# Retention and mixture of depths: the first batch's choice of rows ahead of other loads, its MLP from step 7 in place of step 10

## The chip, the cores and the metric

One core of a Trainium2 chip. The time is the device time of one execution in microseconds; several runs are taken and their median is given. The core's engines work side by side: TensorE (PE, its weight loads are PEld), VectorE (DVE), ScalarE (ACT), GpSimd (POOL) and SyncE (SP), which issues the direct DMA transfers. Each engine takes its instructions in the order in which they are written, and semaphores order them against each other.

## What is computed

Eight batches of 576 rows. The first part is retention: attention without softmax, in which a score is scaled by a power of a factor of its head. The second chooses 128 rows of each batch by a gate score and adds an MLP's result to them.

```python
# retention, B=8 H=8 S=576 D=64
scores = (1/sqrt(D)) * q @ k.T
gamma  = 1 - 2**(-5 - arange(H))
ret    = scores * where(i >= j, gamma**(i - j), 0)
x      = (ret @ v) as (B, S, 512)
# mixture of depths, capacity 128
score  = x @ w_gate
top    = the 128 rows of each batch with the largest score
ye     = relu(x[top] @ w1) @ w2          # 512 -> 1024 -> 512
out    = x;  out[top] += sigmoid(score[top]) * ye
```

## The kernel before

**Steps.** A batch is 9 chunks of 64 rows. A step takes two chunks, so the whole is 36 steps (`NS`) of two chunks in the order of the batches; step 4 (`(NC - 1) // 2`) holds the last chunk of batch 0 and the first of batch 1. A step loads one tile `raw` of 1 MB (q, k, v and natural k for both chunks), tile 0 in two halves. POOL scales v to `vs` (`scaled`). The matmuls of a step are two streams woven together by `matmuls(s)`, two of each in turn: `diagonal(s)` makes the scores `sc_ps` and adds to the running state `u_ps` (copied to `st` by ACT), and `crosswise(s - 1)` makes `y_ps` of the step before, from the masked scores `am` (DVE, `masked`) and the state. One round of four is called an iteration; a full step has 16.

**After the matmuls of a step** come `values(s - 1)` (scale `y_ps` to `xs`, in eight small ACT instructions for the steps in `BUSY`, otherwise in one DVE instruction; then two dot products with the gate's weights on DVE) and `stored(s - 2)`, the stores of `xs` to the output.

**The choice of rows.** When a batch's scores are there, `flatten` (DVE) and `spread` (a matmul with ones and a copy by ACT) lay them out as one `row` on all partitions. `compare` (DVE) counts for each row how many are ahead of it, `one_hot` (DVE) turns the ranks into a selection `hot`, `fetch` turns it into row numbers `idx` by five small matmuls and gathers these rows of the output as `xr` with an indirect DMA on POOL. For batch 0 (and the last two) the first six chunks are laid out and compared ahead of the last three. `gates` makes the sigmoid factor.

**The MLP.** `mlp(b)` transposes `xr` (`turn`, four transposes, then a copy) and puts eight parts on a list: four `up` (16 pairs of matmul passes each) and four `down`. `some(n)` issues n parts at the end of a step; n is chosen so that the list is empty when the next batch is `ready`. The last part scatters the result by an indirect DMA.

**The order around the change** is written by hand. Dictionaries hold what to do in a step: `inner[(s, i)]` before iteration i of the step's matmuls, `first` after them, `soon` and `mid` after `values`, `late` and `then` after the parts of the MLP. TensorE, DVE, ACT and SP follow the order of the program text; POOL's order is left to the scheduler. For batch 0 before:

```python
plan(inner, (s + 1, 12), spread, b, last)          # s = 5
for j in js:
    plan(first, s + 1 + int(j > 2), compare, b, j, last)
plan(first, s + 2, one_hot, b)
plan(inner, (s + 3, 4), fetch, b)
plan(inner, (s + 5, 4), mlp, b)
plan(inner, (s + 5, 13), some, 1)
ready.append(s + 5)
```

**When loads go out.** `pe` counts TensorE's instructions. Each time the count passes the edge of a block of 256 (by `SURE`, 8, more), at most one due piece of the weights (512 KB) and one `raw` tile go out, and only behind the matmul at that place (`behind`); a tile only while fewer than four are loaded ahead of the step (`lead`). With 64 matmuls of four instructions to a step, an edge falls once in about each step. Five tiles are loaded before the first step. The eight pieces of w1 and w2 are due from step 5 to step 12.

Of the kernel before, what the change touches and what calls it, by code (L numbers as in the profile page):

```python
# [21 lines left out]
BEFORE = 65  # L22
SURE = 8
ET = mybir.EngineType
ENGINES = {ET.PE, ET.DVE, ET.Activation, ET.SP}


def layout(NC, HG, cap):
# [11 lines left out]
def kernel(  # L40
# [23 lines left out]
    nc = tc.nc  # L64
    NS = qkvk.shape[0]
    DM = w1.shape[0]
# [4 lines left out]
    NC = 2 * NS // B  # L71
# [3 lines left out]
    W = HG * D  # L75
# [5 lines left out]
    loads = ctx.enter_context(tc.tile_pool(name="loads", bufs=8))  # L81
    work = ctx.enter_context(tc.tile_pool(name="work", bufs=3))
# [8 lines left out]
    chunk = lambda s, a: divmod(2 * s + a, NC)  # L91
    four = lambda ap: ap.rearrange("p (a h d) -> p a h d", a=2, h=HG)

    raw, weights = {}, deque()
    now = {"at": BEFORE, "edge": BLOCK, "load": 0, "step": 0, "quiet": 0}

    def load(behind=None):
        s, now["load"] = now["load"], now["load"] + 1  # L100
        raw[s] = x = loads.tile([P, 4, DM], F32, name="raw")
        n = 4 if s else 2
        for a in range(0, 4, n):
            start(x[:, a : a + n, :],
                  qkvk[s, :, DM * a : DM * (a + n)].rearrange("p (a e) -> p a e", a=n), behind)

    def start(out, in_, behind):
        ins = nc.sync.dma_start(out=out, in_=in_)  # L108
        if behind is not None:
            tc.add_manual_dep(ins.ins, behind.ins.name, mybir.DependencyInfo(  # L110
                mybir.DependencyClass.Sync, mybir.DependencyReason.DATA), reason="behind a fetch")

    def pe(ins, n=4):

        now["at"] += n
        if now["at"] >= now["edge"] + SURE:
            now["edge"] += BLOCK
            lead = now["load"] - now["step"]
            if now["quiet"] and lead > 2:
                now["quiet"] -= 1  # L120
                return ins
            due = weights and weights[0][0] <= now["step"]
            if due:
                start(*weights.popleft()[1:], ins)
            if now["load"] < NS and lead < 4:
                load(ins)
        return ins
# [7 lines left out]

    ctx.enter_context(tc.manual_schedule(engines=ENGINES))
    table = const.tile([P, col["end"]], F32, name="table")
# [16 lines left out]
    for f in range(0, FB, 2):  # L154
        e = slice(P * f, P * f + 2 * P)
# [5 lines left out]
    dec = table[:, : 2 * (NC + 1) * HG].rearrange("p (s c h) -> p s c h", s=2, c=NC + 1)  # L161
# [9 lines left out]
    for _ in range(3):  # L171
# [7 lines left out]

    BUSY = [s for s in range(1, (NC - 1) // 2 + 3) if s != (NC - 1) // 2]
    vs, am, sc_ps, y_ps, u_ps, st, xs, sc = {}, {}, {}, {}, {}, {}, {}, {}
    factor = lambda s, i: dec[:, i, chunk(s, 0)[1] : chunk(s, 0)[1] + 2, :].unsqueeze(3).to_broadcast(
        [P, 2, HG, D])
# [62 lines left out]
    def matmuls(s):  # L248
        a = diagonal(s) if s < NS else iter(())
        b = crosswise(s - 1) if s else iter(())  # L250
        for i in count():
            for f, more in inner.get((s, i), []):
                f(*more)
            some = [f for f in (next(a, None), next(a, None), next(b, None), next(b, None)) if f]
            if not some:
                return
            for f in some:
                f()
# [7 lines left out]
    def values(s):  # L266
        xs[s] = work.tile([P, DM], F32, name="xs", bufs=5)
        if s in BUSY:
            c = chunk(s, 0)[1]
            for a in range(2):  # L270
                for h in range(HG):
                    nc.scalar.activation(out=xs[s][:, hd[a][h]], in_=y_ps[s][:, hd[a][h]],  # L272
                                         func=AF.Copy, scale=dec[:, 1, c + a, h : h + 1])
        else:
            nc.vector.tensor_tensor(out=four(xs[s]), in0=four(y_ps[s]), in1=factor(s, 1),  # L275
                                    op=OP.mult)
        for a in range(2):
# [8 lines left out]
    def stored(s):  # L286
        (b, c), (b1, _) = chunk(s, 0), chunk(s, 1)
        for i, half in enumerate(halves):
            e = slice(W * i, W * i + W)
            if b == b1:  # L290
                nc.sync.dma_start(
                    out=outs[b][C * c : C * c + P, e].rearrange("(a t) e -> t a e", a=2),
                    in_=xs[s][half, :].rearrange("p (a e) -> p a e", a=2))
                continue
            nc.sync.dma_start(out=outs[b][C * c :, e], in_=xs[s][half, :W])
            nc.sync.dma_start(out=outs[b1][:C, e], in_=xs[s][half, W:])

# [123 lines left out]

    inner, first, soon, mid, late, then, ready, parts = {}, {}, {}, {}, {}, {}, [], deque()

    def mlp(b):
        turn(b)
        parts.extend((up, (b, f, 2)) for f in range(0, FB, 2))
        parts.extend((down, (b, part)) for part in range(4))
# [6 lines left out]
    def plan(when, s, f, *a):  # L436
        when.setdefault(s, []).append((f, a))

    for b in range(B):
        end = cuts(b)  # L440

        there = [(NC * b + c - 1) // 2 + 1 for c in end[1:]]
        last = len(there) - 1
        for part, s in enumerate(there):
            plan(soon, s, flatten, b, part)
        for part, s in enumerate(there[:-1]):
            plan(mid, s + 1, spread, b, part)
            for j in own(b, part):
                plan(then if b < B - 1 else mid, s + 1 + int(b == 0 and j > 1), compare, b, j, part)
        if b == B - 1:  # L450
            break
        s = there[-1]
        js = [*range(own(b, last).start), *own(b, last)]
        if b == 0:


            plan(inner, (s + 1, 12), spread, b, last)
            for j in js:
                plan(first, s + 1 + int(j > 2), compare, b, j, last)
            plan(first, s + 2, one_hot, b)  # L460
            plan(inner, (s + 3, 4), fetch, b)
            plan(inner, (s + 5, 4), mlp, b)
            plan(inner, (s + 5, 13), some, 1)
            ready.append(s + 5)
            plan(then, s + 5, gates, b)
            continue


        if last:
            when = 1, (1, 1, 1, 1, 2), 2, 3, 4  # L470
        elif b == 1:
# [15 lines left out]
    for s in range(NS + 1):  # L487
        now["step"] = s
        now["at"] += 1.5
        if s == 1:  # L490
            nc.sync.dma_start(out=wg, in_=spread_out(0, DM, P))
        while now["load"] < min(NS, s + 2):
            load()
        if s + 1 < NS:
            scaled(s + 1)
        matmuls(s)
        if s > 1:
            stored(s - 2)
        for f, a in first.get(s, []):
            f(*a)  # L500
        if s:
            values(s - 1)
        if s == 1:
            nc.vector.tensor_copy(out=place, in_=table[:, col["place"] : col["end"]])
        for f, a in soon.get(s, []) + mid.get(s, []):
            f(*a)

        n = -(-len(parts) // max(1, min([r for r in ready if r > s], default=s + 1) - s))
        some(n if s < NS else len(parts) - 1)
        for f, a in late.get(s, []) + then.get(s, []):  # L510
            f(*a)
    stored(NS - 1)

    b, part = B - 1, len(cuts(B - 1)) - 2
    spread(b, part)
# [72 lines left out]
```

## Time and profile before

| what | value |
|---|---|
| median of 3 runs | 265.66 us (261.38 to 268.25) |
| profiled run, span | 258.1 us |
| PE busy | 225.4 us, 87% of the span |
| DVE busy | 151.2 us, 59% |
| POOL / ACT busy | 59.6 / 59.3 us, 23% each |
| mean granted clock of TensorE | 0.965 |
| moved by DMA | 56.95 MB, mean 221 GB/s |
| gather of batch 0: issue, use by the transposes | 45.41 us, 53.41 us |

In the profile a slice's digit is the busy share in tenths. A gap in front of a group of instructions is given in brackets with what released it; "issue" means that the engine waited for nothing that the profile shows. The shares of busy time are means over stages with different limits: here an early stage with many loads, a long middle in which MLP parts fill the steps, and a tail with the last batch's choice and MLP.

### The profile page before, as it was taken

Reading aid. Unit: us, or ns where it says so; the run is one execution under the profiler, and the core shown is the slowest. Engines: PE = TensorE matmul, PEld = TensorE weight load, DVE = VectorE, ACT = ScalarE, POOL = GpSimd, SP = SyncE. Lnnn points to the kernel's source line nnn. Section 1 sums busy time; section 2 is a strip of 40 time slices with the busy share of each in tenths; the row PEclk is TensorE's granted clock in tenths of the full one; section 3 lists DMA queues with packets and bytes.
Section 4 is the critical chain, followed back from the end, with each engine's and each line's share of the span. In section 5 each row is a group of like instructions: output and inputs, shape, how many; then the busy total and the mean of one; then the engine's idle time right before and its main releaser. Section 6 shows DMA issues by size and latency. Waiting matters only on the chain.

```text
span 258.1 us, 11373 instructions
## 1 busy us (share of the span) xinstructions
PE 225.4 (87%) x5102; PEld 174.8 (68%) x5102; DVE 151.2 (59%) x436; ACT 59.3 (23%) x178; POOL 59.6 (23%) x59
## 2 busy tenths in 40 slices
PE   8565785689889989896999999999999999999991
PEld 3564574579755887555985799568966895784940
DVE  0156788542885536973983699579944861950201
ACT  1125443112510223112221321122211220211200
POOL 3333113312141112133131150413312210101101
PEclk9889979759999999999999999999999999999999
DMA  6999899998666776881778985888876303111101
GB/s 210 403 324 341 260 339 372 379 390 273 212 226 226 234 266 229 289 283 64 235 241 288 301 288 169 263 259 296 285 251 227 99 17 80 44 41 41 43 0 41
DMA packets 20945, 56.95 MB, mean 221 GB/s; under 512 B 2336, under 2 KB 13984, under 8 KB 16416
## 3 DMA queue, kind: packets, MB, share of 16 engines
q1 hardware_dynamic: 19616, 52.02, 59.9%
q0 software_dynamic: 1280, 4.20, 4.6%
q8 instruction: 40, 0.66, 1.0%
q14 instruction: 9, 0.07, 0.1%
HBM read 44.67 MB, written 11.53 MB: 218 GB/s over the span
## 4 chain that ended last, share of the span: by engine, by line
PE 51%; issue 24%; DMA 20%; POOL 2%; POOLq 1%; SPq 0%; DVE 0%
PE h_ps L134 14%; DMA raw<-in_qkvk 10%; PE ye_ps L134 9%; PE u_ps L134 8%; DMA xr<-out,idx 8%; PE sc_ps L134 8%; PE y_ps L134 7%; PE row_ps L134 3%; DMA w_sb<-in_w 2%; PE xg_ps L394 1%; POOL out L419 1%; POOL xr L375 1%; POOL vs L189 1%; POOLq L584 0%; SPq L108 0%
## 5 line engine op out<-in xcount | busy, mean ns | idle before, releaser
L189 POOL TENSOR_TENSOR vs<-raw,table 128x512 f32<-128x512 f32 x36 | 40.1, 1113 | 140.2 <-DMA raw<-in_qkvk 105.1
L134 PE MATMUL h_ps<-xg,w_sb 128*128 128x128 f32 x512 | 61.9, 280 | 0.1
L134 PEld LDWEIGHTS h_ps<-xg,w_sb 128*128 128x128 f32 x512 | 59.6, 195 | 2.2 <-issue 1.2
L134 PE MATMUL ye_ps<-w_sb,hT 128*128 128x512 f32 x128 | 60.1, 605 | 0.0
L134 PE MATMUL u_ps<-vs,raw 64*64 64x64 f32 x1024 | 45.9, 229 | 7.3 <-POOL vs L189 3.1
L262 DVE TENSOR_TENSOR am<-sc_ps,table 128x512 f32<-128x512 f32 x36 | 24.8, 688 | 45.5 <-PE sc_ps L134 26.5
L134 PE MATMUL y_ps<-vs,am 64*64 64x64 f32 x1152 | 46.1, 229 | 5.3 <-issue 4.8
L134 PEld LDWEIGHTS u_ps<-vs,raw 64*64 64x64 f32 x1024 | 37.8, 140 | 18.6 <-issue 12.8
L134 PE MATMUL sc_ps<-raw 64*64 64x64 f32 x1152 | 45.3, 228 | 4.4 <-issue 4.1
L134 PEld LDWEIGHTS sc_ps<-raw 64*64 64x64 f32 x1152 | 40.4, 143 | 9.2 <-issue 7.9
L209 ACT COPY st<-u_ps 128x256 f32<-128x256 f32 x64 | 24.0, 375 | 90.0 <-PE u_ps L134 59.9
L134 PEld LDWEIGHTS y_ps<-vs,am 64*64 64x64 f32 x1152 | 39.5, 141 | 5.4 <-issue 4.8
L134 PE MATMUL y_ps<-st,raw 64*64 64x64 f32 x1024 | 39.9, 226 | 0.9 <-issue 0.8
L283 DVE SCALAR_TENSOR_TENSOR scr<-xs,wg_half 128x256 f32<-128x256 f32 x72 | 34.8, 483 | 6.6 <-ACT xs L272 4.1
L350 DVE SCALAR_TENSOR_TENSOR scr<-row,tok,ahead 128x576 f32<-128x576 f32 (+2 forms) x49 | 36.2, 739 | 2.8 <-ACT row L326 0.8
L134 PEld LDWEIGHTS ye_ps<-w_sb,hT 128*128 128x128 f32 x128 | 22.7, 190 | 21.1 <-issue 20.1
L134 PEld LDWEIGHTS y_ps<-st,raw 64*64 64x64 f32 x1024 | 35.8, 141 | 1.3 <-issue 1.2
L275 DVE TENSOR_TENSOR xs<-y_ps,table 128x512 f32<-128x512 f32 x31 | 21.1, 682 | 7.4 <-PE y_ps L134 7.4
L406 ACT ACTIVATE hT<-h_ps 128x256 f32<-128x256 f32 x32 | 12.3, 384 | 49.1 <-PE h_ps L134 49.1
L343 DVE SCALAR_TENSOR_TENSOR scr<-row,table 128x128 f32<-128x128 f32 (+1 forms) x40 | 12.7, 317 | 14.9 <-ACT row L326 14.2
L418 DVE SCALAR_TENSOR_TENSOR o<-ye_ps,gate,xr 128x512 f32<-128x512 f32 x8 | 6.0, 750 | 24.4 <-issue 12.7
L419 POOL DMA_INDIRECT out<-o,idx x8 | 9.0, 1130 | 35.2 <-DVE o L418 32.5
(32 smaller groups left out, 106.2 us busy)
## 6 DMA issues: line engine op xcount, KB each, us to landing
raw<-in_qkvk SPq DMA_DIRECT2D x35, 1024.0 KB, 5.4
out<-xs SPq DMA_DIRECT2D x64, 128.0 KB, 5.5
w_sb<-in_w SPq DMA_DIRECT2D x8, 512.0 KB, 6.5
raw<-in_qkvk SPq DMA_DIRECT2D x2, 512.0 KB
out<-xs SPq DMA_DIRECT2D x16, 64.0 KB, 6.3
wg<-in_w_gate SPq DMA_DIRECT2D x1, 256.0 KB
table<-in_consts SPq DMA_DIRECT2D x1, 130.5 KB
wg_half<-in_w_gate SPq DMA_DIRECT2D x2, 64.0 KB, 7.3
```

What stands on the lines that cost most here:

```text
L134: return pe(nc.tensor.matmul(out, lhsT, rhs, **more), 4 if lhsT.dtype == F32 else 2)
L189: nc.gpsimd.tensor_tensor(out=four(vs[s]), in0=four(raw[s][:, 2, :]), in1=factor(s, 0), op=OP.mult)
L209: nc.scalar.copy(out=st[b, c], in_=u_ps[b][:, :W])
L262: nc.vector.tensor_tensor(out=am[s], in0=sc_ps[s].rearrange("p (h d) -> p h d", h=H), in1=causal.unsqueeze(1).to_broadcast([P, H, C]), op= ...
L275: nc.vector.tensor_tensor(out=four(xs[s]), in0=four(y_ps[s]), in1=factor(s, 1), op=OP.mult)
L283: nc.vector.scalar_tensor_tensor(scr[:, :W], part, 1.0, wg_half, op0=OP.mult, op1=OP.mult, accum_out=sc[b][:, c : c + 1])
L343: nc.vector.scalar_tensor_tensor(scr[:, :n], row[b][:, P * j : P * j + n], 1.0, eye[:, :n], op0=OP.mult, op1=OP.mult, accum_out=tok[b][:, ...
L350: nc.vector.scalar_tensor_tensor(scr[:, : i1 - i0], row[b][:, i0:i1], tok[b][:, j : j + 1], ahead[:, at + i0 : at + i1], op0=OP.subtract, ...
L375: nc.gpsimd.indirect_dma_start(out=xr[b], out_offset=None, in_=outs[b], in_offset=bass.IndirectOffsetOnAxis(ap=idx[b][:, :1], axis=0))
L406: nc.scalar.activation(out=hT[b][:, f : f + n, :], in_=t[:, :n, :], func=AF.Relu)
L418: nc.vector.scalar_tensor_tensor(o, ye[b], gate[b], xr[b], op0=OP.mult, op1=OP.add)
L419: nc.gpsimd.indirect_dma_start(out=outs[b], out_offset=bass.IndirectOffsetOnAxis(ap=idx[b][:, :1], axis=0), in_=o, in_offset=None)
```

## The change

It puts the choice of batch 0 first. In steps 2 to 5 only half a tile goes out at each block edge, in place of a whole tile (and weights from step 5). The choice is made in steps 4 to 6: the row of the first part in the middle of step 4, the last chunk's values and stores as soon as they are there, the rest of the row and all comparisons within step 6. Two tiles and two weight pieces are sent together at the start of step 6, while DVE compares. The rows are fetched in step 7, and the MLP of batch 0 starts at the end of step 7 in place of step 10, with its eight parts spread over steps 7 to 14. For the later batches the fetch moves behind the step's MLP parts, and the MLPs of batches 1 and 2 come a step later. POOL's order is now written out too, `scaled` stands after the matmuls of a step, and `BUSY` reaches to step 12.

```diff
-ENGINES = {ET.PE, ET.DVE, ET.Activation, ET.SP}
+ENGINES = {ET.PE, ET.DVE, ET.Activation, ET.SP, ET.Pool}
...
+    DONE = (NC - 1) // 2
+    edges = deque([[], [(DONE + 1, 0)], [(DONE + 1, 1)], [(DONE + 2, 0)], [(DONE + 2, 1)],
+                   [], []])
...
+    def half_load(s, i, behind=None):
+
+        if s not in raw:
+            raw[s] = loads.tile([P, 4, DM], F32, name="raw")
+        start(raw[s][:, 2 * i : 2 * i + 2, :],
+              qkvk[s, :, 2 * DM * i : 2 * DM * (i + 1)].rearrange("p (a e) -> p a e", a=2), behind)
+        now["load"] = s + i
...
             now["edge"] += BLOCK
+            now["last"] = ins
+            if edges:
+                for s, i in edges.popleft():
+                    half_load(s, i, ins)
+                return ins
...
-    BUSY = [s for s in range(1, (NC - 1) // 2 + 3) if s != (NC - 1) // 2]
+    BUSY = [s for s in range(1, DONE + 9) if s != DONE]
...
+    def ahead_of(n):
+
+        for _ in range(n):
+            load(now["last"])
+            start(*weights.popleft()[1:], now["last"])
...
-            plan(mid, s + 1, spread, b, part)
+            if b:
+                plan(mid, s + 1, spread, b, part)
+            else:
+                plan(inner, (s + 1, 8), spread, b, part)
...
-            plan(inner, (s + 1, 12), spread, b, last)
+            plan(inner, (s + 1, 4), spread, b, last)
             for j in js:
-                plan(first, s + 1 + int(j > 2), compare, b, j, last)
-            plan(first, s + 2, one_hot, b)
-            plan(inner, (s + 3, 4), fetch, b)
-            plan(inner, (s + 5, 4), mlp, b)
-            plan(inner, (s + 5, 13), some, 1)
-            ready.append(s + 5)
-            plan(then, s + 5, gates, b)
+                plan(inner, (s + 1, 10), compare, b, j, last)
+            plan(inner, (s + 1, 10), one_hot, b)
+            plan(inner, (s + 1, 0), ahead_of, 2)
+            plan(inner, (s + 2, 4), fetch, b)
+            plan(mid, s + 2, mlp, b)
+            plan(mid, s + 2, ahead_of, 1)
+            ready.append(s + 2)
+            plan(then, s + 3, gates, b)
             continue
...
         elif b == 1:
-            when = 1, (1, 1, 1, 2, 2), 2, 3, 4
+            when = 1, (1, 1, 1, 2, 2), 2, 3, 5
         else:
-            when = 1, (1, 1, 2, 2, 3), 3, 4, 5 + int(b > 2)
+            when = 1, (1, 1, 2, 2, 3), 3, 4, 6
...
-        plan(mid, s + when[3], fetch, b)
+        plan(mid if last else late, s + when[3], fetch, b)
...
+        matmuls(s)
         while now["load"] < min(NS, s + 2):
             load()
         if s + 1 < NS:
             scaled(s + 1)
-        matmuls(s)
         if s > 1:
-            stored(s - 2)
+            for span in spans(s - 2)[int(s - 2 == DONE) :]:
+                stored(s - 2, span)
         for f, a in first.get(s, []):
             f(*a)
+        span, *more = spans(s - 1)
         if s:
-            values(s - 1)
+            values(s - 1, span)
+        if s - 1 == DONE:
+            stored(s - 1, span)
...
-        for f, a in soon.get(s, []) + mid.get(s, []):
+        for f, a in soon.get(s, []):
+            f(*a)
+        if s and more:
+            values(s - 1, *more)
+        for f, a in mid.get(s, []):
             f(*a)
```

More of the change, by code (lines that the diff above doesn't have):

```diff
@@ L96 @@
     raw, weights = {}, deque()
+    DONE = (NC - 1) // 2
+    edges = deque([[], [(DONE + 1, 0)], [(DONE + 1, 1)], [(DONE + 2, 0)], [(DONE + 2, 1)],
+                   [], []])
     now = {"at": BEFORE, "edge": BLOCK, "load": 0, "step": 0, "quiet": 0}
-    def load(behind=None):
-        s, now["load"] = now["load"], now["load"] + 1
+    def half_load(s, i, behind=None):
[4 more added lines that the diff above has]
+        now["load"] = s + i
+    def load(behind=None):
+        s = now["load"]
+        if s == 0 or s in raw:
+            for i in range(int(s in raw), 2):
+                half_load(s, i, behind)
+            return
         raw[s] = x = loads.tile([P, 4, DM], F32, name="raw")
[L102 to L105, printed above, removed]
+        start(x, qkvk[s].rearrange("p (a e) -> p a e", a=4), behind)
+        now["load"] = s + 1
     def start(out, in_, behind):
@@ L264, in masked, with spans, values @@
             in1=causal.unsqueeze(1).to_broadcast([P, H, C]), op=OP.mult)
-    def values(s):
-        xs[s] = work.tile([P, DM], F32, name="xs", bufs=5)
+    def spans(s):
+        return [range(2)] if chunk(s, 0)[0] == chunk(s, 1)[0] else [range(1), range(1, 2)]
+    def values(s, span):
+        if s not in xs:
+            xs[s] = work.tile([P, DM], F32, name="xs", bufs=5)
+        b, c = chunk(s, span.start)
         if s in BUSY:
-            c = chunk(s, 0)[1]
-            for a in range(2):
+            for a in span:
                 for h in range(HG):
                     nc.scalar.activation(out=xs[s][:, hd[a][h]], in_=y_ps[s][:, hd[a][h]],
-                                         func=AF.Copy, scale=dec[:, 1, c + a, h : h + 1])
+                                         func=AF.Copy, scale=dec[:, 1, c + a - span.start, h : h + 1])
         else:
-            nc.vector.tensor_tensor(out=four(xs[s]), in0=four(y_ps[s]), in1=factor(s, 1),
-                                    op=OP.mult)
-        for a in range(2):
+            part = slice(span.start, span.stop)
+            nc.vector.tensor_tensor(out=four(xs[s])[:, part], in0=four(y_ps[s])[:, part],
+                                    in1=factor(s, 1)[:, part], op=OP.mult)
+        for a in span:
             b, c = chunk(s, a)
@@ L284, in values, with stored @@
                                            op1=OP.mult, accum_out=sc[b][:, c : c + 1])
-    def stored(s):
-        (b, c), (b1, _) = chunk(s, 0), chunk(s, 1)
+    def stored(s, span):
+        (b, c), n = chunk(s, span.start), len(span)
         for i, half in enumerate(halves):
             e = slice(W * i, W * i + W)
[L290 to L296, printed above, removed]
+            nc.sync.dma_start(
+                out=outs[b][C * c : C * (c + n), e].rearrange("(a t) e -> t a e", a=n),
+                in_=xs[s][half, W * span.start : W * span.stop].rearrange("p (a e) -> p a e", a=n))
     flat, row, tok, rank, hot = {}, {}, {}, {}, {}
@@ L511 @@
             f(*a)
-    stored(NS - 1)
+    for span in spans(NS - 1):
+        stored(NS - 1, span)
     b, part = B - 1, len(cuts(B - 1)) - 2
```

## The prediction, with its working

> **What bounds the kernel now.** I read the slices of the page first, then windows over the early part, then the waits of the matmul engine, then its single gaps in the timeline, and last the engines that release those gaps.
>
> ```profile
> PE   8565785689889989896999999999999999999991
> PEclk9889979759999999999999999999999999999999
> DMA  6999899998666776881778985888876303111101
> GB/s 210 403 324 341 260 339 372 379 390 273 212 226 226 234 266 229 289 283 64 235 241 288 301 288 169 263 259 296 285 251 227 99 17 80 44 41 41 43 0 41
> ```
>
> One slice is 258.1 / 40 = 6.45 us. From about 122 us TensorE is 90% busy or more: what is left there is work. What can be won lies before. Up to 60 us TensorE is 50 to 80% busy while DMA moves 260 to 400 GB/s, and there is a hole in slice 18 (116 to 122 us).
>
> ```profile
> 15.00:18.90 3.90, 2.32 (x128) 2.07 (x129) 2.47 (x6) 0.84 (x3) 1.04 (x1) 1.00 0.86 295
> 49.00:59.40 10.40, 8.88 (x171) 8.01 (x171) 5.64 (x14) 1.23 (x3) 1.74 (x3) 0.51 1.01 374
> ```
>
> The columns are the stretch, its length, busy time of PE, PEld, DVE, ACT, POOL, granted clock, DMA share, GB/s. The first row is step 2: 2.32 us of matmuls in 3.9 us. The second shows that the clock is at half from 49 to 59.4 us, over the very start of the first MLP.
>
> ```profile
> PE y_ps L134 <- issue: 4.4, 4, 1.8
> PE sc_ps L134 <- issue: 3.7, 3, 1.6
> PE idx_ps L134 <- DVE hot L360: 3.0, 2, 1.9
> PE u_ps L134 <- issue: 2.6, 5, 0.6
> ```
>
> These are the waits of the first 75 us. "Issue" is 10.7 us in 12 gaps. Gaps over 0.15 us between 12 and 60 us add up to 14.5 us; three of them and a later one, by the timeline:
>
> ```profile
> 25.25 0.27 PE L134 MATMUL y_ps<-vs,am 64*64 64x64 f32 x1 [1.84 <-issue]
> 43.66 0.36 PE L134 MATMUL idx_ps<-place,hot 128*128 128x1 f16 x5 [1.89 <-DVE hot L360]
> 53.41 1.12 PE L394 MATMUL xg_ps<-table,xr 128*128 128x128 f32 x4 [0.84 <-DMA xr<-out,idx]
> 118.62 0.66 PE L394 MATMUL xg_ps<-table,xr 128*128 128x128 f32 x4 [2.87 <-DMA xr<-out,idx]
> ```
>
> The long issue gaps (1.08, 1.07, 1.84, 1.26, 1.07, 1.57 us) stand about 256 instructions apart; those of 0.5 us stand at the start of a step and end when `am` of the step before is ready. So a step is 2.1 us of matmuls + 0.5 us for `am` + about 1.2 us for instructions, 3.7 to 3.9 us.
>
> [...] The page agrees on the blocks (10,204 TensorE instructions, 40 packets and 0.66 MB on the instruction queue)[...]. [...] The gather agrees: 3.3 us at best, 8.0 us at 45 us, with all of DMA in use. [...] The trace agrees: half clock at about 11 to 14.6, 32 to 35.4 and 49 to 59.4 us, one, one and three windows.
>
> **The change, part by part.**
>
> *Fewer loads in steps 2 to 5.* Half a tile (512 KB) at each of four block edges in place of 1 MB, then at steps 5 and 6 1 MB and 0.5 MB of weights. With 0.25 MB of stores a step then moves 0.75 MB, some 2 us of DMA at 390 GB/s, in place of 3.2 us or more, so a fetch finds free engines. I take the fetch gaps of steps 3 to 5 as gone (1.07, 1.84, 1.26 us). Step 2 keeps its gap, since the first five loads run until 17 us. So step 3 begins at 18.9 us as before, step 4 at 21.0 instead of 22.1.
>
> *The row of the first six chunks moves into step 4 (iteration 8).* Its input is late:
>
> ```profile
> 25.00 0.56 DVE L311 TENSOR_TENSOR flat<-sc,table 128x384 f32<-128x384 f32 x1
> 36.15 0.41 DVE L350 SCALAR_TENSOR_TENSOR scr<-row,tok,ahead 128x192 f32<-128x192 f32 x1
> 40.38 0.28 DVE L343 SCALAR_TENSOR_TENSOR scr<-row,table 128x128 f32<-128x128 f32 x1
> 40.71 0.82 DVE L350 SCALAR_TENSOR_TENSOR scr<-row,tok,ahead 128x576 f32<-128x576 f32 x1
> 42.77 0.82 DVE L360 TENSOR_TENSOR hot<-table,rank 128x640 f16<-128x640 f32 x1
> ```
>
> `flat` ended at 25.56, 3.3 us after step 3's matmuls (1.75 us of ACT, two dot products, itself). Moved with step 3 it is ready at 24.2; TensorE gets there at 22.5 and waits 1.7 us. With 0.84 us for the row and 0.75 us of matmuls, step 5 begins at 25.8 (before: 27.6).
>
> *Tile 6 becomes a late load.* By the count of the code, its second half (v and natural k) goes out at the fifth edge, matmul 28 of 56 in step 5, about 26.7 us. No 512 KB load alone is in the trace; 1 MB takes this:
>
> ```profile
> DMA to landing us min/median/max: 5.0/5.4/8.5
> ```
>
> Less 1.25 us for half the bytes gives 3.75; [...] I take 3.5: landed 30.2, then 1.04 us for `vs` on POOL. Step 6 starts at 31.4, not at 28.2: a new wait of 3.2 us (2.5 to 5).
>
> *The comparisons move into step 6, ahead of `masked(6)`.* The row is at 31.9 + 0.63, its copy done at 33.0. On DVE: three partial comparisons 1.35 us, two tokens with their full comparisons 2.2, the sum of ranks 0.2, `hot` 0.75: 4.5 us, so 37.5. Behind them in the queue is `masked(6)`, 0.69 us, and the first `y` matmuls of step 7 wait for it: 38.3. TensorE has finished step 6 at 34.0: 4.3 us of new wait, in place of the 1.89 us for `hot`. The two loads and two weight pieces of step 6 (3 MB, 7.7 us at 390 GB/s) pass in this time; what they do to instruction fetches lies beside the wait.
>
> *Gather and MLP.* In step 7 the index is out at 39.3. GpSimd is now in written order too: the gather stands ahead of `vs` of tile 8. It shares DMA with tile 9 and a third piece (1.5 MB); between the best 3.3 and the 8.0 of before I take 4.8, landed 44.3. Step 7's matmuls end at 40.6: wait 3.7 us. The turn starts at 44.3 and not 53.4, but before had done steps 8, 9 and a quarter of 10 by then: 2.25 x 2.1 = 4.7 us. Gain here: 53.4 - 44.3 - 4.7 = 4.4 us. Before pays half clock until 59.4 us, some 3 us after the turn; with the idle time above I give the change the same.
>
> *Steps 7 to 14.* One part of the MLP per step in place of two: 2.1 + 1.95 us of TensorE, 1.75 MB = 4.4 us of DMA until the weights are in. From 39.5 us to step 13 it is 11.3 MB = 29 us, done at 70 with latency; TensorE would be at 71. Balanced, with tile s+2 asked for in step s: I charge 2 us for `vs` waits and 1.5 us for fetch gaps. Copies of `y` on ACT until step 12 add 1.75 us to ACT per step, 2.9 of 4.1 with states and relu: hidden, and DVE gets 0.68 free.
>
> *Later batches.* The fetch moves behind a part of 1.98 us, which hides the waits for `hot` at 74.9 and 109.6 us (1.11, 1.24), and batches 1 and 2 get two full steps for their gathers, which removes the 2.87 at 118.6; I also count out the wait for a state at 67.4 us (0.68), which sits behind two parts of an MLP's relu on ACT where one will be. Sum 5.9 us. Split stores, stores of batch 0 a step earlier and `values` in two pieces add a fixed cost of some 0.3 us beside DVE's waits: nothing.
>
> Sum: 4.4 + 5.9 - 3.5 = 6.8, say 7 us of 265.7: 258.7 us.
>
> **Rivals.** *Back to even, 264 us.* The gather comes into the 1.5 MB burst and takes 8.0 us again (+3.2), and fetch gaps in steps 8 to 13 are 4 us instead of 1.5 (+2.5): gain 1. For: DMA demand of 1.75 MB a step. Against: between 55 and 65 us matmuls of the MLP ran at 5.00 of 5 us busy beside 348 GB/s.
>
> *Slower, 274 us.* On top, the three waits of steps 6 and 7 (11 us within 16) keep the clock at half for three more windows, 1.7 us each (+5), and `vs` is 1 us late in five of the steps 8 to 14 (+5): 264 + 10. For: a lead of two tiles where before had three, and the half clock of before at just such a place. Against: MLP parts lengthen each step to 4 us, longer cover than in steps 2 to 9 of before.
>
> *Much faster, 251 us.* The half load lands as fast as it is needed (2.7), the gather takes 3.3 (1.5), no fetch gaps or late tiles (3.5): 7.7 more. For: DMA is nearly idle in steps 3 to 5. Against: the least landing seen for any direct load.
>
> **How the numbers follow.** Forecast 0.52, much faster 0.18, even 0.15, slower 0.15. Three timings of before spread from 261.4 to 268.3 us, so a tenth of the forecast's cases falls within 2% (above 260.3): faster 0.47 + 0.18 = 0.65, within 2% 0.05 + 0.15 = 0.20, slower 0.15. The range takes in most of the fast and the even case: 250.5 to 267.5.
>
> **What would show it.** Right: 12 to 60 us shows issue gaps under 4 us in all; a wait of `u_ps` for `vs` at about 28 to 31 us; a wait of `y_ps` for `am` of 3 to 4.5 us in step 7; the first turn near 44 us; no wait for `hot` or `xr` after 60 us. Wrong: issue gaps of 1 us stay in steps 3 to 5 with half the loads (the cause is then not the loads); the gather takes 7 us or more; `vs` waits of over 1 us recur in steps 8 to 14; half clock lasts beyond two windows after the turn.

## The result: slower by 4%, and the profile after

The changed kernel takes 274.97 us in the median (272.11 to 277.30, 4 runs) against 263.52 us for the kernel before on the same chip (260.66 to 268.25): a ratio of 1.042, interval 1.033 to 1.051. The forecast was 258.7 us; the time came out at the rival called "Slower, 274 us". Some executions of one and the same kernel come out over 1.5% above its fastest; the ratios here and below leave these out, the medians don't, and of the profiles only that of e10 is of such an execution. The profiled execution spans 271.2 us, 13.1 us more than the 258.1 before.

The slices of the page after, 6.78 us each, are to be read beside those of before:

```profile
PE   8545544696888889996999999999999999999992
PEclk9999957789799999999999999999999999999998
DMA  6986389649999983887887765668867612111101
GB/s 207 391 333 201 107 284 360 224 148 268 314 318 331 340 278 114 297 241 258 265 260 235 272 194 160 255 213 276 262 201 262 207 44 81 41 39 39 41 0 39
```

Where before moved 260 to 400 GB/s from slice 1 to slice 8, DMA now falls to 201 and 107 GB/s (20 to 34 us), and again to 224 and 148 (47 to 61 us). TensorE is 40 to 60% busy from 7 to 47 us. The stretches of both kernels in the same grid (columns as in the prediction), before first:

```profile
0.00:20.00 20.00, 13.63 (x349) 9.86 (x350) 4.79 (x10) 4.71 (x14) 7.29 (x12) 0.91 0.86 312
20.00:35.00 15.00, 10.31 (x412) 8.88 (x411) 10.81 (x32) 6.23 (x26) 3.62 (x4) 0.89 0.95 312
35.00:50.00 15.00, 8.70 (x383) 7.54 (x386) 10.68 (x34) 5.42 (x23) 4.25 (x4) 0.96 1.02 362
50.00:65.00 15.00, 13.71 (x205) 12.23 (x197) 5.86 (x15) 3.01 (x8) 2.40 (x2) 0.70 0.91 327
65.00:80.00 15.00, 13.21 (x368) 9.34 (x371) 11.25 (x33) 3.95 (x10) 3.64 (x3) 1.00 0.73 242
```

and after:

```profile
0.00:20.00 20.00, 12.18 (x319) 8.13 (x323) 4.40 (x9) 3.76 (x9) 7.22 (x12) 1.00 0.84 309
20.00:35.00 15.00, 8.21 (x354) 6.68 (x350) 8.20 (x29) 6.91 (x29) 1.62 (x2) 0.93 0.54 167
35.00:50.00 15.00, 8.78 (x242) 7.61 (x246) 8.13 (x29) 3.04 (x13) 4.01 (x4) 0.61 0.81 277
50.00:65.00 15.00, 12.21 (x318) 11.22 (x312) 4.43 (x13) 8.19 (x29) 1.30 (x2) 0.88 0.70 224
65.00:80.00 15.00, 11.68 (x273) 9.38 (x271) 7.39 (x23) 7.30 (x30) 3.25 (x3) 0.89 0.93 313
```

GB/s times length, summed, gives 24.9 MB moved by 80 us before and 20.9 MB after. At the 390 GB/s that the early stage reached, 4 MB are 10 us. Nothing of the work needs fewer bytes: 56.95 MB move in both kernels. By itself this sum doesn't name a cause: loads go out behind matmuls, so a kernel that is behind for any reason has also moved less. Of the difference from 20 to 35 us half is due to the half loads: without them (e5, below) the changed kernel moves 244 GB/s there.

The waits of TensorE in the first 75 us after, and single gaps of the timeline:

```profile
PE u_ps L153 <- POOL vs L208: 10.1, 5, 4.2
PE y_ps L153 <- issue: 4.8, 4, 2.5
```

```profile
32.07 0.27 PE L153 MATMUL y_ps<-vs,am 64*64 64x64 f32 x2 [2.48 <-issue]
37.73 0.37 PE L153 MATMUL u_ps<-vs,raw 64*64 64x64 f32 x2 [4.17 <-POOL vs L208]
46.33 0.27 PE L153 MATMUL y_ps<-vs,am 64*64 64x64 f32 x2 [2.85 <-DVE am L281]
51.77 0.66 PE L415 MATMUL xg_ps<-table,xr 128*128 128x128 f32 x4 [1.22 <-DMA xr<-out,idx]
68.57 0.27 PE L153 MATMUL u_ps<-vs,raw 64*64 64x64 f32 x2 [2.65 <-POOL vs L208]
```

The 4.17 us are the second half of tile 6, the 2.85 us the comparisons ahead of `masked(6)`, the 1.22 us the gather, the 2.65 us tile 10, which was sent at 58.3 us and could be used at 67.5. (A "turn" is the start of a batch's transposes; the first is that of batch 0.) In the whole span TensorE waits 14.1 us for `vs`, 11 more than before. The first turn starts at 51.77 us: 1.6 us ahead of before, but with 2.25 steps (4.7 us) less done, so 3 us behind at equal work. The second turn, at 94.96 us against 82.94 and one step further, is 9.9 us behind. Then the distance grows slowly: the turn of batch 3 comes after the same 25 steps and three MLPs in both (156.09 against 145.48), 10.6 us behind, the end 13.1.

### The profile page after: what moved, and what is told of

Read it like the earlier page. It is cut to its first block, busy times and chain, and to the rows that moved or that the text cites. A ratio compares the mean times of both kernels' runs of the same rounds, so it can differ in the third digit from the quotient of the medians.

```text
span 271.2 us, 11436 instructions
## 1 busy us (share of the span) xinstructions
PE 228.8 (84%) x5102; PEld 177.2 (65%) x5102; DVE 150.1 (55%) x434; ACT 69.5 (26%) x226; POOL 59.2 (22%) x59
## 2 busy tenths in 40 slices
DMA packets 21233, 56.95 MB, mean 210 GB/s; under 512 B 2368, under 2 KB 14016, under 8 KB 16960
## 4 chain that ended last, share of the span: by engine, by line
PE 44%; issue 23%; DMA 20%; POOL 5%; DVE 3%; ACT 2%; SPq 1%; POOLq 1%; ACTq 0%
DMA raw<-in_qkvk 20%; PE h_ps L153 13%; PE ye_ps L153 9%; PE u_ps L153 7%; PE y_ps L153 6%; PE sc_ps L153 6%; POOL vs L208 3%; PE row_ps L153 2%; DVE scr L371 1%; ACT xs L296 1%; POOL out L440 1%; SPq L122 1%; POOL xr L396 1%; SPq L166 1%; PE xg_ps L415 0%
## 5 line engine op out<-in xcount | busy, mean ns | idle before, releaser
L153 PE MATMUL h_ps<-xg,w_sb 128*128 128x128 f32 x512 | 64.0, 285 | 1.6 <-ACT xg L416 0.9
L153 PEld LDWEIGHTS h_ps<-xg,w_sb 128*128 128x128 f32 x512 | 61.2, 198 | 4.1 <-issue 2.0
L153 PE MATMUL u_ps<-vs,raw 64*64 64x64 f32 x1024 | 45.3, 228 | 17.1 <-POOL vs L208 14.1
L153 PE MATMUL y_ps<-vs,am 64*64 64x64 f32 x1152 | 47.6, 227 | 10.3 <-issue 6.9
L153 PEld LDWEIGHTS u_ps<-vs,raw 64*64 64x64 f32 x1024 | 37.6, 140 | 26.7 <-POOL vs L208 18.8
L281 DVE TENSOR_TENSOR am<-sc_ps,table 128x512 f32<-128x512 f32 x36 | 24.8, 688 | 53.8 <-PE sc_ps L153 43.5
L153 PE MATMUL sc_ps<-raw 64*64 64x64 f32 x1152 | 46.5, 226 | 4.1 <-issue 3.7
L153 PE MATMUL y_ps<-st,raw 64*64 64x64 f32 x1024 | 39.5, 224 | 0.6 <-issue 0.4
L371 DVE SCALAR_TENSOR_TENSOR scr<-row,tok,ahead 128x576 f32<-128x576 f32 (+2 forms) x49 | 35.6, 727 | 6.3 <-ACT row L347 3.7
L153 PEld LDWEIGHTS ye_ps<-w_sb,hT 128*128 128x128 f32 x128 | 22.7, 189 | 21.4 <-issue 20.1
L300 DVE TENSOR_TENSOR xs<-y_ps,table 128x512 f32<-128x512 f32 (+1 forms) x29 | 17.6, 607 | 5.5 <-PE y_ps L153 5.5
L296 ACT ACTIVATE xs<-y_ps,table 128x64 f32<-128x64 f32 x88 | 19.2, 335 | 1.2 <-PE y_ps L153 1.0
L364 DVE SCALAR_TENSOR_TENSOR scr<-row,table 128x128 f32<-128x128 f32 (+1 forms) x40 | 15.0, 374 | 7.0 <-ACT row L347 6.3
```

Source lines behind the costliest of these rows:

```text
L153: return pe(nc.tensor.matmul(out, lhsT, rhs, **more), 4 if lhsT.dtype == F32 else 2)
L281: nc.vector.tensor_tensor(out=am[s], in0=sc_ps[s].rearrange("p (h d) -> p h d", h=H), in1=causal.unsqueeze(1).to_broadcast([P, H, C]), op= ...
L300: nc.vector.tensor_tensor(out=four(xs[s])[:, part], in0=four(y_ps[s])[:, part], in1=factor(s, 1)[:, part], op=OP.mult)
L364: nc.vector.scalar_tensor_tensor(scr[:, :n], row[b][:, P * j : P * j + n], 1.0, eye[:, :n], op0=OP.mult, op1=OP.mult, accum_out=tok[b][:, ...
L371: nc.vector.scalar_tensor_tensor(scr[:, : i1 - i0], row[b][:, i0:i1], tok[b][:, j : j + 1], ahead[:, at + i0 : at + i1], op0=OP.subtract, ...
```

## The experiments

Each ratio is against runs of the kernel before on the same chip. MB at 80 us is worked out as above; the first turn is the first of the transposes in the timeline.

| run | edit | median us | ratio, interval | MB at 80 us | first turn us |
|---|---|---|---|---|---|
| e1_lead3 | changed, a tile more in step 7 | 270.2 | 1.037, 1.023 to 1.052 | 22.5 | 51.2 |
| e2_early_tiles | changed, tiles 5 and 6 whole at edges 2 and 3 | 273.3 | 1.049, 1.036 to 1.063 | 21.4 | 49.7 |
| e3_before_later | before, with the later batches' part | 261.8 | 1.011, 0.997 to 1.025 | 24.8 | 51.7 |
| e4_no_tiles | before, no tile loaded after tile 4 | 260.9 (one run) | | | 50.6 |
| e5_no_hold | changed, no half loads | 265.8 | 1.024, 1.013 to 1.035 | 21.8 | 55.2 |
| e6_before_hold | before, with half loads (one of them sent twice) | 272.2 | 1.049, 1.042 to 1.057 | 21.1 | 65.8 |
| e7_mask_first | changed, `masked(6)` ahead of comparisons | 268.5 | 1.033, 1.023 to 1.043 | 20.5 | 54.8 |
| e8_after_no_later | changed, without the later batches' part | 274.1 | 1.055, 1.044 to 1.066 | 20.3 | 53.5 |
| e9_mlp_step8 | e5, MLP from step 8 | 263.3 | 1.019, 1.008 to 1.031 | 24.3 | 52.9 |
| e10_no_burst | e5, no loads sent together | 261.2 | 1.005, 1.000 to 1.009 | 22.5 | 50.7 |
| e11_both | e5 with both | 255.2 | 0.977, 0.969 to 0.985 | 25.1 | 50.5 |
| e12_both_mask | e11 with e7's edit | 266.4 | 1.021, 1.013 to 1.029 | 23.6 | 53.9 |

### Are the half loads the cause? Added, and taken away

The kernel before with half loads (the list, and a `half_load` as in the change, are left out of the cut):

```diff
             now["edge"] += BLOCK
+            hold = edges.popleft() if edges else None
+            for s, i in hold or []:
+                half_load(s, i, ins)
...
-            if now["load"] < NS and lead < 4:
+            if now["load"] < NS and lead < 4 and hold is None:
```

> The kernel before with only the list of half loads added: at the second to fifth edge half a tile in place of a tile, none at the sixth and seventh (weights still go out when due, and a tile that the next step needs is sent at its start). Theory backlog: this alone makes it slower by 6 to 12 us, to 268 to 274, with waits of u_ps for vs at steps 6 to 10. Rival order: holding back costs less than 3 us because the steps 2 to 5 win their instruction gaps back.

It is 4.9% slower: as much as the whole change. Its waits for tiles over the whole span, the longest of them in its timeline, and its loads of half a tile:

```profile
PE u_ps L148 <- POOL vs L203: 20.4, 10, 6.3
PE u_ps L148 <- DMA raw<-in_qkvk: 9.2, 1, 9.2
37.64 0.37 PE L148 MATMUL u_ps<-vs,raw 64*64 64x64 f32 x2 [9.25 <-DMA raw<-in_qkvk]
raw<-in_qkvk SPq DMA_DIRECT2D x7, 512.0 KB, 4.2
```

The instruction gaps of steps 3 and 4 are indeed smaller (0.52 and 0.75 us, for 1.07 and 1.84), and the scores of step 5 begin 1.7 us earlier than before (26.43 for 28.09 us), about what the prediction had for this (1.8). Then 29.6 us of waits for tiles follow. But the run holds more than the half loads of the change. It has seven loads of half a tile (two are tile 0's) where the change has six, and moves 57.47 MB: the second half of tile 6 goes out at 26.27 us, because the next step needs it, and again behind the fifth edge, at 32.91 us. `vs` was made from the first copy by 32.88 us, and the matmuls wait for the second until 37.64: 4.8 of the 9.25 us. Nor does it send two tiles together in step 6 as the change does, to make up for those held back. So 4.9% is not the price of the half loads in the change; the next run is the better witness.

The changed kernel with the list empty:

```diff
-    edges = deque([[], [(DONE + 1, 0)], [(DONE + 1, 1)], [(DONE + 2, 0)], [(DONE + 2, 1)],
-                   [], []])
+    edges = deque([])
```

> The changed kernel without the list of half loads: from the second edge on a tile goes out at each edge as in the kernel before; early choice, early MLP and the later batches' part stay. Theory backlog: holding tiles back leaves DMA idle (197 and 79 GB/s at 25 to 35 us) and at 80 us some 4 MB behind the kernel before (20.9 against 24.9 MB), which at 390 GB/s is 10 us that no later order gives back; here DMA moves over 24 MB by 80 us and the time falls by 8 to 13 us, to between 258 and 265. Rival order: the loss comes from the early choice and MLP themselves (DVE ahead of masked(6), one MLP part a step, half clock); then the time stays over 268.

From 1.042 to 1.024: a bit over 40% of the loss comes back (the two intervals just touch), and 265.8 lies just over the range that the backlog theory gave. Waits for `vs` are 2.3 us in the whole span, in place of 14.1, nearly all of it at the start. But the bytes are not there by 80 us (21.8 MB, not 24), for another reason, seen in a gap and a stretch of this kernel:

```profile
55.23 1.11 PE L414 MATMUL xg_ps<-table,xr 128*128 128x128 f32 x4 [6.95 <-DMA xr<-out,idx]
```

```profile
50.00:65.00 15.00, 9.10 (x162) 8.29 (x165) 2.09 (x8) 3.78 (x15) 1.04 (x1) 0.64 0.39 146
```

The gather, issued at 46.0 us, lands after 9.2 us, in which 3.3 MB of direct transfers move. While TensorE waits for it, no edge is passed, so no load goes out: 146 GB/s.

### Is it only where the held tiles go out?

> The changed kernel with tile 5 sent whole at the second edge and tile 6 whole at the third; nothing at the fourth and fifth. Theory late half: the 4.2 us wait for vs of tile 6 at 37.7 us is due to its second half going out behind the fifth edge; here it is gone, the row of the last three chunks is out 4 us earlier and the first turn starts near 48 instead of 51.8 us: time 3 to 4 us less than the changed kernel. Rival loads delay instructions: the whole tiles bring issue gaps of 1 to 1.8 us in steps 3 and 4 (0.75 and 1.07 in the changed kernel), and at most 1.5 us is won.

```diff
-    edges = deque([[], [(DONE + 1, 0)], [(DONE + 1, 1)], [(DONE + 2, 0)], [(DONE + 2, 1)],
-                   [], []])
+    edges = deque([[], [(DONE + 1, 0), (DONE + 1, 1)], [(DONE + 2, 0), (DONE + 2, 1)], [], [],
+                   [], []])
```

The wait for tile 6 goes, as expected, and the first turn is 2.1 us earlier (49.7 us, 48 expected), but the time isn't less (272.0 against 271.2 us of span). The gaps of steps 3 and 4 are 0.80 and 1.30 us, so the rival's 1 to 1.8 holds for one of them. The wait stands one tile further on, and later ones are longer:

```profile
42.31 0.37 PE L153 MATMUL u_ps<-vs,raw 64*64 64x64 f32 x2 [4.72 <-POOL vs L208]
80.25 0.37 PE L153 MATMUL u_ps<-vs,raw 64*64 64x64 f32 x2 [3.60 <-POOL vs L208]
```

> The changed kernel with one tile more sent in step 7 (tiles 9 and 10 instead of 9 alone), so that tiles stay three ahead of the step afterwards, as in the kernel before. Theory lead: the loss after the first turn (43.2 us from turn 0 to turn 1, with 7.1 us of gaps) comes from tiles asked for only two steps ahead; then the waits of u_ps for vs after 60 us (2.65, 0.71, 0.87, 2.25 us and smaller, 6.6 in all) fall below 2 us and the time falls by 4 to 6 us to about 268. Rival bandwidth: DMA cannot bring 1.75 MB a step in any order; the waits stay above 4 us in sum and the time is within 1.5 us of the changed kernel.

```diff
-            plan(mid, s + 2, ahead_of, 1)
+            plan(mid, s + 2, ahead_of, 1, 1)     # one tile more
```

With a tile more of lead the waits for `vs` fall from 14.1 to 6.8 us in the whole span (the 4.6 us of tile 6 stay), but issue gaps grow from 13.5 to 17.4 us: 1.91, 1.26, 1.66 and 0.84 us between 67 and 91 us. The profile is 2.6 us shorter, below the 4 us expected, and the intervals of the ratios (1.037 and 1.042) overlap. In the waits both theories hold in part: with the earlier request they shrink, and gaps for instructions grow by half as much. In time a gain is not shown.

### What the instruction gaps are worth

> The kernel before without the loads of tiles 5 to 35: the steps from 5 on read the first five tiles again. Its output is not the reference's; stores and weights stay. Theory floor: [...] issue gaps of 0.7 to 1.1 us stay in steps 3 to 5 (20 to 31 us) with hardly any traffic. Theory of the prediction: the bulk loads cause these gaps; without them the gaps of steps 3 to 5 are gone (below 0.3 us).

```diff
+        if s > 4:
+            raw[s] = raw[s % 5]
+            return
```

Loads cause the gaps: from 21 to 50 us no issue gap over 0.3 us is left. Yet the time is that of the kernel before (260.9, a single run, against a median of 261.85), and step 8's scores start at 43.96 us, against 43.95. From the scores of step 3 to those of step 8 it wins only 2.3 us. Up to 2 us more may be hidden there, since from 20 to 44 us its clock was at half for 7.2 us, against 3.4 before. What stands in the gaps' place in this kernel:

```profile
27.81 0.91 PE L137 MATMUL row_ps<-flat,ones 128*128 128x384 f32 x2 [1.31 <-DVE flat L314]
43.67 0.36 PE L137 MATMUL idx_ps<-place,hot 128*128 128x1 f16 x5 [1.47 <-DVE hot L363]
```

With a second wait for `flat` (1.02 us), one for `am` (0.99) and waits for states of 0.5 to 0.9 us in four steps (ACT) this is some 7 us. In these steps DVE and ACT keep almost the same pace as the instruction blocks, so removing one of the two limits uncovers the other.

### The comparisons ahead of masked(6)

> The changed kernel with the comparisons and the selection of batch 0 after masked(6) on DVE, not ahead of it. Theory chain: what ends last in steps 6 and 7 is the chain row, comparisons, hot, index, gather, transposes; the wait of y_ps for am (2.9 us) goes and comes back as a wait for hot or xr, and hot comes 0.7 us later: time within 1.5 us of the changed kernel. Rival queue: masked(6) behind the comparisons costs TensorE its 2.9 us outright: 2 to 3 us faster than the changed kernel.

```diff
-                plan(inner, (s + 1, 10), compare, b, j, last)
-            plan(inner, (s + 1, 10), one_hot, b)
+                plan(inner, (s + 1, 13), compare, b, j, last)
+            plan(inner, (s + 1, 13), one_hot, b)
```

In the changed kernel DVE ran `hot` from 44.85 us and `masked(6)` behind it from 45.60 us. With the edit the wait for `am` goes and comes back, as the chain theory has it, and the wait for `xr` grows too, since here the gather takes 6.8 us:

```profile
47.04 0.38 PE L153 MATMUL idx_ps<-place,hot 128*128 128x1 f16 x5 [2.75 <-DVE hot L381]
54.75 1.12 PE L415 MATMUL xg_ps<-table,xr 128*128 128x128 f32 x4 [4.56 <-DMA xr<-out,idx]
```

At the second turn this kernel is 2 us behind the changed one (96.95 against 94.96). It is faster in the end all the same (profile 267.1 against 271.2), from work that the edit doesn't touch, and the intervals of the ratios overlap. So the run says nothing for the queue theory; the same edit made on the best version says the contrary:

> The version with neither half loads nor loads sent together and the MLP from the end of step 8, now with the comparisons of batch 0 after masked(6) on DVE. Theory chain: the wait of y_ps for am (3.6 us) goes and comes back as a wait of the index matmuls for hot, two to three matmul groups later, since the fetch stands in iteration 4 of step 7; hot comes 0.7 us later: within 1.5 us of that version (255.2). Rival queue: masked(6) behind the comparisons costs its wait outright, as the 4 us between the changed kernel and its variant with this edit would have it: 2 to 4 us faster, 251 to 253.

It is 11 us slower than e11 (described below), which neither theory gave. The wait for `am` of 3.58 us became a wait for `hot` of the same size:

```profile
45.99 0.38 PE L152 MATMUL idx_ps<-place,hot 128*128 128x1 f16 x5 [3.58 <-DVE hot L380]
```

the first turn came 3.4 us later (53.88 against 50.48), beside 17 us of half clock between 33 and 54 us in place of 7, and the rest came later, in unchanged work. Two stretches, from the turn of batch 3 to that of batch 5, with the same instructions on TensorE: e11 first, then e12.

```profile
142.79:196.40 53.61, 52.93 (x1278) 41.74 (x1277) 40.47 (x118) 12.73 (x35) 14.69 (x13) 1.00 0.73 243
```

```profile
146.80:203.29 56.49, 54.31 (x1277) 42.45 (x1276) 41.20 (x118) 12.63 (x35) 14.30 (x13) 1.00 0.72 231
```

This stretch takes 53.1 to 54.0 us in before, e5, e7, e8, e9, e10 and e11, and 56.0 to 56.5 us in the changed kernel, e1, e2 and e12; e3 (54.8) and e6 (55.8) lie between. Half of the difference is idle time in gaps of 0.4 to 0.7 us, half longer matmuls. It makes up 2.6 of the 13.1 us that the changed kernel lost, and what decides it was not found. The same edit thus took the ratio from 1.042 to 1.033 and from 0.977 to 1.021: what a single edit does to the time here can be more than the waits that it touches, and the other differences of a few per cent in the table are to be read with that in mind.

### The later batches

> The changed kernel with the later batches as before (fetch ahead of the MLP parts, MLP of batches 1 and 2 a step earlier). Theory of the prediction: the later part is worth 3 to 5 us, so this is slower than the changed kernel by as much, 276 to 279, with waits for hot and xr back after 75 us. Rival: the later part is worth under 1.5 us, since waits for vs and instructions take their place; within 1.5 us of the changed kernel.

```diff
-            when = 1, (1, 1, 1, 2, 2), 2, 3, 5
+            when = 1, (1, 1, 1, 2, 2), 2, 3, 4
...
-        plan(mid if last else late, s + when[3], fetch, b)
+        plan(mid, s + when[3], fetch, b)
```

> The kernel before with only the later batches' part of the change: fetch behind the parts of the MLP, MLP of batches 1 and 2 a step later. Theory of the prediction: the waits for hot at 74.9 and 109.6 us (1.1 and 1.2) and for xr at 118.6 us (2.9) go, nothing comes in their place: 3 to 5 us faster than before. Rival: a later gather and scatter stand in GpSimd's queue ahead of a tile's vs, and u_ps waits for vs appear by 1 to 2 us each: no gain.

Undone in the changed kernel, the waits return, here over the whole span:

```profile
PE xg_ps L415 <- DMA xr<-out,idx: 11.9, 4, 4.5
PE idx_ps L153 <- DVE hot L381: 4.0, 3, 1.4
```

They were 1.5 us for `xr` and none worth a line for `hot`. The profile is 2.7 us longer, just under the 3 to 5 us expected, but the intervals of the ratios (1.055 and 1.042) overlap. Added to the kernel before, the waits for `xr` and for the later `hot` go as well; the time gives no verdict (ratio 0.997 to 1.025, equal medians). So the waits were read rightly; the 3 to 5 us in time are not shown.

### The gather, and a version that beats both

> The changed kernel without the list of half loads, and with the MLP of batch 0 from the end of step 8 in place of step 7 (seven steps for its eight parts). Theory bare gather: without the held loads the gather takes 9.2 us (46.0 to 55.2) and TensorE waits 7.0 us for it because only one step's rest lies between fetch and transposes; a step more hides 3 to 4 us of it: xr wait 3 to 4 us, time 3 to 4 us less than without the list alone (265.8), to about 262. Rival: the wait only moves (tiles not asked for while TensorE waits, instruction gaps): within 1.5 us of 265.8.

> The changed kernel without the list of half loads and without the tiles and weights sent together in steps 6 and 7: both go out one per edge as in the kernel before. Theory bare gather: the gather is slow because of what was sent just ahead of it; with about 2.5 MB less sent in steps 6 and 7 it lands in 6 to 7 us instead of 9.2, the wait for xr falls to 4 to 5 us and the time to about 263. Rival: the queue is as full with one tile and one piece at each edge (8.0 us in the kernel before): the wait stays at 6 us or more and the time within 1.5 us of 265.8.

> Both at once: no list of half loads, no loads sent together, MLP from the end of step 8; early comparisons and the later batches' part stay. If the hold and the bare gather are the two causes, this is back at the kernel before or up to 1% faster: 256 to 261 us. Rival order: comparisons ahead of masked(6) and one MLP part a step cost 3 us or more by themselves: 263 or more.

All three start from the kernel without half loads. The two edits are:

```diff
-            plan(mid, s + 2, mlp, b)                 # e9, e11
+            plan(mid, s + 3, mlp, b)
...
-            plan(inner, (s + 1, 0), ahead_of, 2)     # e10, e11
-            plan(mid, s + 2, ahead_of, 1)
```

A step more between fetch and transposes (e9) leaves 1.40 us of the 6.95 us wait, less than the 3 to 4 expected; the median falls by 2.5 us, but the interval (1.008 to 1.031) overlaps that of e5. Without loads sent together (e10) the gather lands in 5.3 us, sooner than either theory had it, the wait is 3.4 us, and the median falls by 4.6 us, to the kernel before. With both, the gather takes 4.7 us and TensorE does not wait for it (0.3 us over the whole span). Two stretches of this version:

```profile
50.00:65.00 15.00, 12.30 (x316) 11.27 (x311) 5.80 (x16) 8.46 (x31) 2.13 (x2) 1.00 1.01 356
65.00:80.00 15.00, 12.87 (x360) 9.39 (x361) 10.73 (x35) 7.32 (x31) 4.38 (x4) 0.93 1.00 361
```

Its ratio is 0.977 (0.969 to 0.985), the only one wholly under 1. It keeps the early comparisons and has the MLP from the end of step 8 in place of step 10, and by 80 us it has moved 25.1 MB, a little more than before. So the loss goes in three pieces when these are taken away one after the other: the half loads (1.042 to 1.024), the loads sent together just ahead of the gather (to 1.005), and the MLP with no step between gather and use (to 0.977).

## Why the prediction was wrong, step by step

Forecast were 6.8 us won, the profile shows 13.1 lost. Of these 19.9 us, 7.5 are missing at the first turn (51.77 us in place of 44.3), 5.1 between the first two turns (1.7 lost by the forecast with its share of the later batches, 6.8 measured), and 7.3 after the second (4.1 won by the forecast, 3.2 lost).

**The term left out: bytes put off.** This is the step that failed first. The working priced the held loads by the gaps that they save, never by the DMA time that is lost. DMA moved 167 instead of 312 GB/s from 20 to 35 us, 2.2 MB or 5.6 us; half of it comes back without the half loads. In the changed kernel TensorE waits 14.1 us for tiles, of which the working had 3.2 for tile 6 and 2 later; without the half loads (e5) it waits 2.3, and 1.8 of the 4.2% come back. The rest comes back when the gather is freed too (e10 and e11).

**Fewer loads in steps 2 to 5: right alone, lost in the change.** Half loads by themselves win 1.7 us by step 5 (e6), for 1.8 predicted. In the changed kernel step 5 began at 28.6 us, not at 25.8. Step 3 began 0.9 us later than before, behind a gap of 2.46 us in step 2. Such gaps in step 2 are 1.1 to 2.8 us long in the runs, even with the same instructions up to there. From step 3 to step 5 it takes 8.7 us, as before: the gap of step 3 stayed at 1.07, that of step 4 fell from 1.84 to 0.75, and 0.75 went to the wait for `flat`, which was foreseen at 1.7. The gap of step 5 grew to 2.48 us although only some 0.8 MB were sent from 25 us on. It is as long without half loads (2.42 in e5, 3.31 in e11), and its cause stays open. The prediction held that gaps which stay with half the loads would clear the loads; e4 shows that in the kernel before the loads cause them. It also took each gap for time won; by e4 all of them together were worth 2.3 us, some 4 at the most, over five steps.

**"Steps 7 to 14: balanced": mis-sized.** It took DMA to be busy without a break from 39.5 us on, 11.3 MB in 29 us, and charged 3.5 us. But loads go out behind TensorE's matmuls, and TensorE had stood still for 2.5, 4.2 and 2.9 us by 46.3 us. Step 13 started at 84.7 us in place of 71, 7.5 of the 13.7 us already lost at the first turn. Between the first two turns there are 43.2 us where the work of before (29.5 us with 3.25 fewer steps of 2.1) would make 36.4: 6.8 us in place of 3.5, of which 4.2 are waits for `vs`. The prediction's ground for a balance, matmuls 5.00 of 5 us busy beside 348 GB/s, is the stretch of before from 55 to 60 us, where the granted clock was 0.59, so it doesn't show whether the loads keep up at full clock.

**Tile 6 a late load: right.** 4.17 us measured, 3.2 predicted. `vs` could start 4.2 us after the issue, but that went out at 32.4 us and not at 26.7, because step 5 began late and the edge stood behind the 2.48 us gap. The half loads of the change took 3.9 to 4.4 us to land, for 3.5 taken; 3.5 was the author's estimate, 0.25 under the 3.75 that follows from the least landing of 1 MB before (5.0 us).

**Comparisons ahead of masked(6): right in kind**, 2.85 us for 4.3. **Gather: right, with luck.** 3.7 us to land, 4.8 predicted, and 1.2 us of wait for 3.7. In e7 and e8, with the same held loads, the gather took 6.8 us: there the next tile and piece went out 0.7 us after it, here 1.4. Without the held loads it took 9.2 us (e5), and 5.3 when nothing was sent together either (e10).

**Later batches: the waits right, the gain not shown.** After the second turn the waits of before for `hot` (1.24) and `xr` (2.87) are all but gone, but there are a wait for `vs` of 2.25 us and gaps of 0.4 to 0.7 us in their place, and the stretch that takes 2.6 us longer for a cause not found.

**Clock.** The change spends six windows of 3.4 us at half clock ahead of the last 3 us (33.0 to 43.2, 46.6 to 50.0, 53.5 to 56.9 and 70.5 to 73.9 us), against five before (11.3 to 14.7, 31.8 to 35.2 and 48.9 to 59.1 us); TensorE's busy time grows by 3.4 us. That is one more window, not the three of the rival. That waits keep the clock at half was the author's estimate: in the 3.4 us ahead of the three falls of before TensorE was 46 to 55% busy, ahead of the four of the change 17 to 44%, and no run shows what sets the clock.

The rival at 274 us had the right places, late tiles with a lead of two and the clock, for chances of 0.15. But its gather of 8.0 us and two of its three windows did not come, so that its sum came out is in part luck; what it lacked was the DMA time given away at 20 to 35 us. Not tried by themselves: the written order of POOL, `scaled` behind the matmuls, and `values` on ACT up to step 12. The version e11 has all three and is faster than before.

## What to carry to other kernels

Where a stage keeps DMA busy almost throughout (0.95 of the time from 20 to 35 us before), holding a load back to shorten a wait is a loan: before counting gaps, count megabytes moved by a fixed time, in both kernels, and say when the rest is to be moved. Where loads go out behind another engine's progress, each wait of that engine stops them too (146 GB/s around the 6.95 us wait of e5), so give the wait something to hide it (a step between gather and use) and let the loads keep their lead. Before a gap is counted as time won, look for the engine that would end last without it. And where a part of a change is added to another kernel, count what that kernel then moves: e6 moved 0.5 MB too many.

## What was not expected of the hardware

**Instruction blocks.** The page of before has 5,102 matmuls, as many weight loads, and 40 packets of 16 KB on the instruction queue, so about 256 TensorE instructions to a packet. In the records of single transfers of both kernels such a packet takes 0.9 to 1.6 us. In steps 2 to 5 of the changed kernel the packets end at 16.43, 20.45, 23.84 and 30.69 us, and TensorE goes on at 17.83, 21.73, 25.10 and 32.07 us, 1.3 to 1.4 us after each. Beside loads the gaps that end there are up to 2.5 us long; with no tile loaded (e4) no issue gap over 0.3 us is left from 21 to 50 us.

The packet of step 5 started at 29.74 us, 4.6 us after the block before it was begun. When it was asked for, the trace doesn't tell, so what held it back is not shown, and neither is how loads delay such a packet: that it finds free engines when less is loaded was the prediction's estimate. This packet did not go last: eight packets of 1 KB of stores issued at 25.9 and 26.5 us ran only from 30.68 us on, when it had ended.

**The gather.** It brings the same 256 KB each time, and in five runs it took the longer, the more the direct transfers moved between its issue and its landing: 3.7 us beside 0.2 MB (changed kernel), 4.7 beside 0.7 (e11), 5.3 beside 0.9 (e10), 8.0 beside 2.7 (before) and 9.2 beside 3.3 (e5).
